# Opening of a fused SSD and MLP kernel: second weight slice in halves between ramps, the long running sum moved forward, one load released a step sooner

## The chip, the core and the metric

The kernel runs on one core of a Trainium2 chip. Its engines are TensorE (PE in the profile; its weight loads have a row of their own, PEld), VectorE (DVE), ScalarE (ACT), GpSimd (POOL) and SyncE (SP), whose queue issues nearly all DMAs here. The metric is the device time of one execution in microseconds; the median of the runs is compared.

## What is computed

First a state-space attention block (4 batches, 8 heads, 768 tokens, head dimension 32, state 16), then an MLP over the 3072 tokens that come out of it (256 wide, 2048 hidden). The core of the reference, cut:

```python
log_a = np.log(np.clip(a, 1e-06, 1.0))
for c in range(nc):                                   # chunks of tokens
    cum = np.cumsum(la, axis=-1)
    L = np.exp(cum[:, :, :, None] - cum[:, :, None, :]) * causal
    M = np.einsum('bhin,bhjn->bhij', Cc, Bc) * L
    y[:, :, sl] = M @ xc + (Cc @ state) * np.exp(cum)[..., None]
    state = np.exp(np.sum(la, -1)) * state + ...      # decayed B^T x of the chunk
x = y.transpose(0, 2, 1, 3).reshape(B * S, H * D)
h = x @ w_in                                          # 3072x256 @ 256x2048
g = h * np.clip(h + 3.0, 0.0, 6.0) / 6.0
out = g @ w_out                                       # 2048x256
```

The two weight matrices arrive as 64-bit floats. [...]

## The kernel before

**Stages.** The tokens are worked on in six chunks of 128 per batch (512 tokens a chunk over the four batches). An opening computes the attention of chunk 0. Then, for each chunk k, comes its MLP, with the attention of the next chunk woven in. The MLP's first half runs over 16 units f of 128 hidden columns. In chunk 0 a unit is `mlp_in` (L711): two matmuls of 128x512 in float32 into one of four PSUM banks (tag `f0` to `f3`, bank f % 4), then a ramp on ACT (`ramp`, L819: relu of h/6 + 1/2 into gT) and the product with h on DVE (`times_ramp`, L824). A bank is free for unit f + 4 when L824 of unit f has read it. `first_out` (L837) multiplies gT with w_out, after the sixteen units.

**Weights.** w_in and w_out come in eight slices of 1 MB, `load_w(0)` to `load_w(7)` (L157), through three buffers named raw; slices 0 to 3 are w_in, and slice i serves the units 4i to 4i + 3. The SP queue issues the loads in order. Load 1 is held back by a memset of one column on DVE (L154): it is called in `multiply` (L642, four products of chunk 0's decays with its scores) behind the second of the four products. Load 2 is held back by a copy of one column on POOL (L156) that reads what load 1 brought.

Decoding a slice, 128x1024 numbers, takes on ACT a copy of the top 16 bits (ws, L246) and two passes that make the exponent out of them (L270, L273), and on DVE the significand in two passes (wm, L249 and L253), two masks (we and ws, L263 and L265), an OR of sign and exponent (L277) and the product that writes the slice (L287). `decode(i)` is a generator of five steps, and `weights(i, n)` advances it by n. Slice 1 is decoded by `decode_halves` (L201): the same passes, with those on the exponent, the OR and the product cut into two halves of 512 columns (L211, L217, L220, L222, L229, L231; the significand L212 and L224 is whole). The first half holds the columns of units 4 and 5, the second those of units 6 and 7.

**The order.** It is written out by hand, and each engine executes its instructions in that order. The main part of the opening ends with `decode_halves(1)`, and so all of slice 1's passes stand ahead of unit 0's ramp on ACT, and ahead of unit 0's L824 on DVE. The 16 units follow:

```python
    for i in range(2, NP + 2):
        for j in range(5):
            weave.setdefault(4 * i - 8 + j, []).append(i)
...
                mlp_in(k, f, lambda: [weights(i, 1) for i in late])
```

so slice 2's copy stands behind unit 0, its masks behind unit 1, and so on to its product in unit 4, ahead of that unit's L824; slices 3, 4 and 5 follow four units apart each.

**The running sum.** `add_up` (L319) is a scan on DVE over the logarithms of a, one row per batch and head. The first 256 columns are summed in the opening. The other 512 are summed behind the 16 units of chunk 0, and what reads them follows: `spread_cum` (L368), `store_rows` (L336, L338), `load_eto` (L358) and `load_decay` (L351) send them through DMA to the later chunks' tiles.

The functions follow as the program had them before, with the line numbers of the profile.

Of the kernel before, what the change touches and what calls it, by code (L numbers as in the profile page):

```python
# [8 lines left out]
FP32 = mybir.dt.float32  # L9
U32 = mybir.dt.uint32  # L10
U16 = mybir.dt.uint16
BF16 = mybir.dt.bfloat16
F32R = mybir.dt.float32r
AF = mybir.ActivationFunctionType
ALU = mybir.AluOpType
# [6 lines left out]
def kernel(  # L22
# [24 lines left out]
    nc = tc.nc  # L47
# [7 lines left out]
    NK = DM // P  # L55
# [78 lines left out]
    NP = 4  # L134
    FP = NF // NP
    w_in = [const.tile([P, NK, FP * P], FP32, name="w_in", tag=f"w{i}") for i in range(NP)]
# [33 lines left out]
    def conceal_in(t, pattern):  # L170
# [16 lines left out]
    bias_hi = const.tile([P, 1], FP32, name="bias_hi")  # L187
    nc.vector.memset(bias_hi, 1151.0 * 2 ** 7)
    bias_lo = const.tile([P, 1], FP32, name="bias_lo")
# [4 lines left out]
        out=head, in_=head, pattern=[[-2 * N, NQ], [-N, 2]], compare_op=ALU.is_ge,  # L194
        fill=0.0, base=0, channel_multiplier=1)
    nc.gpsimd.affine_select(
        out=head, in_=head, pattern=[[2 * N, NQ], [N, 2]], compare_op=ALU.is_ge,
# [3 lines left out]
    def decode_halves(i):  # L201

        n, cut = NK * FP * P, FP * P // 2
        top = raws[i].bitcast(U16).rearrange("p (k f w) -> p k f w", k=NK, w=4)[..., 3]
        lo, hi = (raws[i].rearrange("p (n w) -> p n w", w=2)[:, :, w] for w in range(2))
        s = att.tile([P, n], U16, name="ws").rearrange("p (k f) -> p k f", k=NK)
        e = att.tile([P, n], U16, name="we").rearrange("p (k f) -> p k f", k=NK)
        m = att.tile([P, n], U32, name="wm")
        halves = [slice(h * cut, (h + 1) * cut) for h in range(2)]
        for h in halves:  # L210
            nc.scalar.copy(out=s[:, :, h], in_=top[:, :, h])  # L211
        nc.vector.tensor_scalar(  # L212
            out=m, in0=hi, scalar1=0xFFFFF, scalar2=0x100000,
            op0=ALU.bitwise_and, op1=ALU.bitwise_or)
        for h in halves:
            for t, mask in ((e, 0x7FF0), (s, 0x8000)):
                nc.vector.tensor_scalar(  # L217
                    out=t[:, :, h], in0=s[:, :, h], scalar1=mask, scalar2=None,
                    op0=ALU.bitwise_and)
            nc.scalar.activation(  # L220
                e[:, :, h].bitcast(BF16), e[:, :, h], AF.Relu, bias=bias_hi, scale=-8.0)
            nc.scalar.activation(  # L222
                e[:, :, h], e[:, :, h].bitcast(BF16), AF.Relu, bias=bias_lo, scale=-1.0)
        nc.vector.scalar_tensor_tensor(  # L224
            out=m.bitcast(FP32), in0=lo, scalar=2.0 ** -32, in1=m, op0=ALU.mult, op1=ALU.add)
        load_w(i + NRAW)
        m = m.bitcast(FP32).rearrange("p (k f) -> p k f", k=NK)
        for h in halves:
            nc.vector.tensor_tensor(  # L229
                out=e[:, :, h], in0=e[:, :, h], in1=s[:, :, h], op=ALU.bitwise_or)  # L230
            nc.vector.scalar_tensor_tensor(  # L231
                out=w_in[i][:, :, h], in0=m[:, :, h], scalar=2.0 ** -20,
                in1=e[:, :, h].bitcast(BF16), op0=ALU.mult, op1=ALU.mult)

    def decode(i):

        n = NK * FP * P  # L240
        top = raws[i].bitcast(U16).rearrange("p (n w) -> p n w", w=4)[:, :, 3]
        lo, hi = (raws[i].rearrange("p (n w) -> p n w", w=2)[:, :, w] for w in range(2))
        s = att.tile([P, n], U16, name="ws")
        e = att.tile([P, n], U16, name="we")
        m = att.tile([P, n], U32, name="wm")
        nc.scalar.copy(out=s, in_=top)  # L246

        def significand():
            nc.vector.tensor_scalar(  # L249
                out=m, in0=hi, scalar1=0xFFFFF, scalar2=0x100000,  # L250
                op0=ALU.bitwise_and, op1=ALU.bitwise_or)
            yield
            nc.vector.scalar_tensor_tensor(  # L253
                out=m.bitcast(FP32), in0=lo, scalar=2.0 ** -32, in1=m, op0=ALU.mult,
                op1=ALU.add)
            yield

        parts_m = significand()
        if i == 0:
            next(parts_m)  # L260
            next(parts_m)
        yield
        nc.vector.tensor_scalar(  # L263
            out=e, in0=s, scalar1=0x7FF0, scalar2=None, op0=ALU.bitwise_and)
        nc.vector.tensor_scalar(  # L265
            out=s, in0=s, scalar1=0x8000, scalar2=None, op0=ALU.bitwise_and)
        if i:
            next(parts_m)
        yield
        nc.scalar.activation(e.bitcast(BF16), e, AF.Relu, bias=bias_hi, scale=-8.0)  # L270
        next(parts_m, None)
        yield
        nc.scalar.activation(e, e.bitcast(BF16), AF.Relu, bias=bias_lo, scale=-1.0)  # L273
        if i > 1 and i + NRAW < 2 * NP:
            load_w(i + NRAW)
        yield
        nc.vector.tensor_tensor(out=e, in0=e, in1=s, op=ALU.bitwise_or)  # L277
        if i == 0:
            yield
        m, e = m.bitcast(FP32), e.bitcast(BF16)  # L280
        if i < NP:
            dst = w_in[i]
            m, e = (t.rearrange("p (k f) -> p k f", k=NK) for t in (m, e))
        else:
            dst = w_out[:, (i - NP) * FP:(i - NP + 1) * FP, :]
            m, e = (t.rearrange("p (k f) -> p k f", k=FP) for t in (m, e))
        nc.vector.scalar_tensor_tensor(  # L287
            out=dst, in0=m, scalar=2.0 ** -20, in1=e, op0=ALU.mult, op1=ALU.mult)
# [29 lines left out]
    def add_up(sl):  # L318
        nc.vector.tensor_tensor_scan(  # L319
            out=cum[:, sl], data0=run.rearrange("g c p -> g (c p)")[:, sl], data1=a_sb[:, sl],  # L320
            initial=0.0, op0=ALU.mult, op1=ALU.add)
# [165 lines left out]
    def turn_b(c):  # L487

        t_ps = turn_ps(c, 1)
        transposes(c, 1, t_ps)  # L490
        (nc.scalar.copy if c else nc.vector.tensor_copy)(out=turned(c)[0], in_=t_ps)
# [136 lines left out]
    def multiply(c):  # L628

        if 0 < c < TURN:  # L630
            take(c)
        if c <= TURN:
            mids[c] = mid = att.tile([P, NB, 2 * D], FP32, name="mid", bufs=1)
        if c == 0:
            for t in range(2):
                nc.scalar.activation(
                    mid[:, :, t * D:(t + 1) * D], sps[c][0][:, :, t * D:(t + 1) * D], AF.Copy,
                    scale=parity[:, t:t + 1])
            take(c)
        for q in (2, 0, 1, 3) if c >= TURN else range(NQ):  # L640
            hs = slice(2 * q, 2 * q + 2)
            nc.vector.tensor_tensor(  # L642
                out=Ls[c][:, :, hs], in0=Ls[c][:, :, hs], in1=cbs[c][q], op=ALU.mult)
            if c == 0 and q == 1:
                load_w(1)
            if 0 < c <= TURN and q == 1:
                new_state(mid, sps[c][0], tmps[c])
# [63 lines left out]
    def mlp_in(k, f, between):  # L711
        h = ps.tile([P, TB], FP32, name="h", tag=f"f{f % 4}")
        for j in range(NK):
            n = TB // (1 + (f * NK + j >= NF * NK - 0))
            for t in range(0, TB, n):
                nc.tensor.matmul(  # L716
                    out=h[:, t:t + n], lhsT=w_in[f // FP][:, j, f % FP * P:(f % FP + 1) * P],
                    rhs=yTs[k][:, j].rearrange("p b i -> p (b i)")[:, t:t + n],
                    start=(j == 0 and t == 0), stop=True, skip_group_check=True)
        ramp(k, f, h)  # L720
        between()
        times_ramp(k, f, h)
# [427 lines left out]
    def weights(i, n):  # L1150
        for _ in range(n):
            next(parts[i], None)


    def diff(c, *bs):
        for part in (diff_less, diff_pick):
            for b in bs:
                part(c, b)
# [18 lines left out]
            load_x(0)  # L1177
    first_eto()
    turn_b(0)
    diff(1, 0)  # L1180
    diff(1, 1)
    weights(0, 1)
# [20 lines left out]
    renew(0)  # L1203
    mix(0)
    keep(0)
    decode_halves(1)
    load_bc(1)
    load_x(1)


    weave, t_parts = {}, split_sum()
    for i in range(2, NP + 2):
        for j in range(5):
            weave.setdefault(4 * i - 8 + j, []).append(i)
    weave[NF - 1].append(NP + 2)
    for k in range(NC):
        gTs[k] = ffn.tile([P, NF, TB], FP32, name="gT")
        c, ahead = k + 1, k + 2
        if k == 0:
            for f in range(NF):  # L1220
                late = [i for i in weave.get(f, []) if f == 4 * i - 4]
                mlp_in(k, f, lambda: [weights(i, 1) for i in late])
                for i in weave.get(f, []):
                    if i not in late:
                        weights(i, 1)
                if f in (6, 8):
                    diff_exp(c, f // 2 - 3)
            weights(NP + 1, 1)
            add_up(ends_at[1])
            cum_q = spread_cum()  # L1230
            store_rows()
            load_eto(c)
# [180 lines left out]
```

## Time and profile before

| | us |
|---|---|
| median of 3 runs (lowest, highest) | 338.36 (338.15, 338.55) |
| profiled execution, own time | 337.99 |
| its span, first instruction to last | 336.2 |
| PE busy | 328.2 (98% of the span) |
| DVE busy | 262.7 (78%) |
| ACT busy | 207.8 (62%) |
| POOL busy | 131.3 (39%) |

The profile is of one execution. The granted TensorE clock was 1.00 in it. All times below are microseconds from the start of the span. A row of a timeline has the start, the duration (of the whole group, where it ends in a count), engine, line, operation, output and inputs; in square brackets stands the idle time before it with what ended it. A row of the chain of waits has start, duration, and what the end of the program hung on in that time. Matmuls in float32 leave two records each, so a unit of two matmuls has four.

### The profile page before, as it was taken

Reading aid. Unit: us, or ns where it says so; the run is one execution under the profiler, and the core shown is the slowest. Engines: PE = TensorE matmul, PEld = TensorE weight load, DVE = VectorE, ACT = ScalarE, POOL = GpSimd, SP = SyncE. Lnnn points to the kernel's source line nnn. Section 1 sums busy time; section 2 is a strip of 40 time slices with the busy share of each in tenths; the row PEclk is TensorE's granted clock in tenths of the full one; section 3 lists DMA queues with packets and bytes.
Section 4 is the critical chain, followed back from the end, with each engine's and each line's share of the span. In section 5 each row is a group of like instructions: output and inputs, shape, how many; then the busy total and the mean of one; then the engine's idle time right before and its main releaser. Section 6 shows DMA issues by size and latency. Waiting matters only on the chain.

```text
span 336.2 us, 8336 instructions
## 1 busy us (share of the span) xinstructions
PE 328.2 (98%) x3361; PEld 263.7 (78%) x3361; DVE 262.7 (78%) x419; ACT 207.8 (62%) x450; POOL 131.3 (39%) x126
## 2 busy tenths in 40 slices
PE   6999999999999999999999999999999999999995
PEld 3653358888878888888888888888888888899995
DVE  7787999788699729769949558938678958599973
ACT  3777877658976571677662477643487221677661
POOL 2100000172364799079983078771058750000000
PEclk9999999999999999999999999999999999999999
DMA  6869990492980215239107257100141001110001
GB/s 102 170 220 306 120 338 16 112 136 63 205 108 0 59 26 138 39 59 88 40 2 164 36 79 71 33 4 10 28 72 18 2 4 17 29 20 0 2 0 62
DMA packets 90277, 25.22 MB, mean 75 GB/s; under 512 B 82880, under 2 KB 86624, under 8 KB 89728
## 3 DMA queue, kind: packets, MB, share of 16 engines
q1 hardware_dynamic: 89664, 24.57, 38.4%
q8 instruction: 26, 0.43, 0.6%
q10 hardware_dynamic: 576, 0.13, 0.2%
q14 instruction: 11, 0.09, 0.1%
HBM read 21.33 MB, written 3.29 MB: 73 GB/s over the span
## 4 chain that ended last, share of the span: by engine, by line
PE 81%; DVE 8%; DMA 6%; ACT 2%; issue 1%; SPq 0%; POOL 0%; DVEq 0%; POOLq 0%
PE h L780 29%; PE wc L1028 8%; PE o L837 8%; PE wb L1028 8%; PE wa L1028 7%; PE o_end L992 6%; DMA raw<-in_moe_w_in_dram 5%; PE h L716 4%; PE wb L1036 3%; DVE gT L824 2%; PE y L690 2%; DVE q_part L920 2%; PE y L556 2%; PE cb L587 1%; DVE w_part L752 1%
## 5 line engine op out<-in xcount | busy, mean ns | idle before, releaser
L824 DVE SCALAR_TENSOR_TENSOR gT<-gT,h 128x512 f32<-128x512 f32 x96 | 64.7, 683 | 24.8 <-ACT gT L819 23.3
L819 ACT ACTIVATE gT<-h,half 128x512 f32<-128x512 f32 x96 | 65.0, 685 | 21.5 <-PE h L780 21.4
L800 ACT ACTIVATE h<-h 128x512 f32<-128x512 f32 x66 | 38.2, 585 | 38.0 <-PE h L780 37.7
L780 PE MATMUL h<-y_hi,w_part 128*128 128x512 f32 x160 | 51.6, 407 | 0.5 <-DVE gT L824 0.5
L780 PE MATMUL h<-y_less,w_part 128*128 128x512 f32 x160 | 50.2, 399 | 0.0
L780 PE MATMUL h<-y_lo,w_part 128*128 128x512 f32 x160 | 49.4, 395 | 0.0
L883 POOL TENSOR_TENSOR s<-gT 128x512 f32<-128x512 f32 x16 | 24.9, 1555 | 50.8 <-DVE gT L824 50.8
L780 PEld LDWEIGHTS h<-y_hi,w_part 128*128 128x128 f32 x160 | 29.9, 188 | 7.8 <-DVE gT L824 1.2
L780 PEld LDWEIGHTS h<-y_lo,w_part 128*128 128x128 f32 x160 | 30.0, 188 | 7.3
L780 PEld LDWEIGHTS h<-y_less,w_part 128*128 128x128 f32 x160 | 29.1, 188 | 6.0 <-ACT h L800 0.2
L445 ACT ACTIVATE L<-L,cum_n 128x64 f32<-128x64 f32 x128 | 31.7, 336 | 0.7 <-POOL L L173 0.7
L716 PE MATMUL h<-yT,w_in 128*128 128x512 f32 x64 | 28.8, 600 | 1.2 <-DVE gT L824 1.2
L837 PE MATMUL o<-w_out,gT 128*128 128x256 f32 x128 | 28.8, 381 | 0.0
L837 PEld LDWEIGHTS o<-w_out,gT 128*128 128x128 f32 x128 | 24.1, 190 | 3.8 <-issue 0.5
L716 PEld LDWEIGHTS h<-yT,w_in 128*128 128x128 f32 x64 | 11.6, 189 | 17.6 <-issue 11.5
L883 POOL TENSOR_TENSOR gT<-gT 128x512 f32<-128x512 f32 x16 | 23.9, 1500 | 0.7
L173 POOL TENSOR_SCALAR_AFFINE_SELECT L<-L 64x1024 f32<-64x1024 f32 (+1 forms) x16 | 19.9, 1249 | 7.5 <-DMA L<-cum_d 7.2
L920 DVE TENSOR_TENSOR q_part<-gT,q_part 128x256 fp32r<-128x256 f32 x24 | 21.4, 921 | 0.0
L992 PE MATMUL o_end<-v_pair,g_pair 128*128 128x256 f32 x120 | 21.0, 281 | 0.0
L883 POOL TENSOR_TENSOR s<-s,gT 128x512 f32<-128x512 f32 x16 | 20.5, 1289 | 0.0
L992 PEld LDWEIGHTS o_end<-v_pair,g_pair 128*128 128x128 f32 x120 | 18.8, 189 | 1.2
L456 POOL TENSOR_TENSOR bs<-B,L 128x128 f32<-128x128 f32 x24 | 11.7, 507 | 17.8 <-ACT L L445 12.1
(173 smaller groups left out, 615.7 us busy)
## 6 DMA issues: line engine op xcount, KB each, us to landing
raw<-in_moe_w_in_dram SPq DMA_DIRECT2D x4, 1024.0 KB
raw<-in_moe_w_out_dram SPq DMA_DIRECT2D x4, 1024.0 KB
L<-cum_d SPq DMA_DIRECT2D x8, 512.0 KB
xt<-in_x_dram SPq DMA_DIRECT2D x6, 512.0 KB
out_dram<-back SPq DMA_DIRECT2D x128, 16.0 KB
B<-in_B_dram SPq DMA_DIRECT2D x6, 256.0 KB
eto<-cum_e SPq DMA_DIRECT2D x20, 64.0 KB
pairs<-in_C_dram SPq DMA_DIRECT2D x36, 32.0 KB
```

Of the source, the lines that this page charges most:

```text
L173: nc.gpsimd.affine_select(out=t[rows], in_=t[rows], pattern=pattern, compare_op=ALU.is_ge, fill=-1e5, base=base, channel_multiplier=-1)
L445: nc.scalar.activation(Ls[c][:, b, h], Ls[c][:, b, h], AF.Exp, bias=cum_n[:, c, g:g + 1])
L716: nc.tensor.matmul(out=h[:, t:t + n], lhsT=w_in[f // FP][:, j, f % FP * P:(f % FP + 1) * P], rhs=yTs[k][:, j].rearrange("p b i -> p (b i)" ...
L780: nc.tensor.matmul(out=hs_[k, f], lhsT=w[j][:, f % FP * P:(f % FP + 1) * P], rhs=y[:, j], start=(start and j == 0), stop=True, skip_group_ ...
L800: nc.scalar.activation(h, h, AF.Copy, scale=1.0 / EPS + 1.0)
L819: nc.scalar.activation(gTs[k][:, f], h, AF.Relu, bias=half, scale=1.0 / 6.0)
L824: nc.vector.scalar_tensor_tensor(out=g, in0=g, scalar=1.0, in1=h, op0=ALU.min, op1=ALU.mult)
L837: nc.tensor.matmul(out=o[:, b % 2], lhsT=gTs[0][:, f, b * P:(b + 1) * P], rhs=w_out[:, f], start=(f == 0 and b % 2 == 0), stop=True, skip_ ...
L883: nc.gpsimd.tensor_tensor(out=o, in0=p_, in1=q_, op=op)
L920: nc.vector.tensor_tensor(out=l[:, j], in0=g[:, j], in1=h[:, j].bitcast(FP32), op=ALU.subtract)
L992: nc.tensor.matmul(out=ends_["cross" if n == 2 else "squares"][b], lhsT=g_parts[t][n][:, b * P:(b + 1) * P], rhs=w, start=(t == 0 and b < ...
L1028: nc.tensor.matmul(out=bank[:, slot], lhsT=lhs[:, j], rhs=rhs[:, j], start=(clear and j == 0), stop=True, skip_group_check=True)
```

## The change

Five edits in the same kernel. Names and line numbers are those of before.

1. `load_w(1)`, and with it the memset that releases the second load, is called behind the first of the four products in `multiply`.
2. The scan of the last 512 columns, `add_up(ends_at[1])`, is called in the opening, behind the copy of bT (L491) and ahead of slice 0's decoding, and no longer behind the 16 units.
3. `decode_halves` becomes a generator. Its exponent passes on ACT and its OR and product on DVE are done for the first half, then it pauses; unit 0's ramp and product follow, then the second half's.
4. Slice 2's steps move within the units: the copy (L246) and the first significand pass (L249) to unit 2, between its ramp and its L824; the masks to unit 3; the exponent passes and the second significand pass behind unit 3; OR and product in unit 4 as before.
5. In `decode(2)` the first significand pass stands in the first step, ahead of the masks.

On ACT the order of the pieces concerned was: both halves' exponent passes, ramp 0, copy of slice 2, ramps 1 and 2, exponent pass of slice 2, ramp 3, second pass. It becomes: first half's passes, ramp 0, second half's passes, ramps 1 and 2, copy of slice 2, ramp 3, the two passes of slice 2. On DVE it was: half, half, L824 of units 0 and 1, masks of slice 2, significand, unit 2, significand, unit 3, OR, product, units 4 and 5. It becomes: half, unit 0, half, unit 1, significand, unit 2, masks, unit 3, significand, OR, product, units 4 and 5. PE and POOL keep their order, and the SP queue keeps the order of its DMAs. The new line numbers are 8 to 13 higher: 256, 260, 271, 273, 285, 295 for `decode`, 226, 231, 234, 218, 220 for the halves, 650 for the four products, 827 and 832 for ramp and product of a unit.

```diff
@@ decode_halves
+        def exponents(h):
+            nc.scalar.activation(
+                e[:, :, h].bitcast(BF16), e[:, :, h], AF.Relu, bias=bias_hi, scale=-8.0)
+            nc.scalar.activation(
+                e[:, :, h], e[:, :, h].bitcast(BF16), AF.Relu, bias=bias_lo, scale=-1.0)
+
+        def result(h):
+            nc.vector.tensor_tensor(
+                out=e[:, :, h], in0=e[:, :, h], in1=s[:, :, h], op=ALU.bitwise_or)
+            nc.vector.scalar_tensor_tensor(
+                out=w_in[i][:, :, h], in0=m.bitcast(FP32).rearrange("p (k f) -> p k f", k=NK)[:, :, h],
+                scalar=2.0 ** -20, in1=e[:, :, h].bitcast(BF16), op0=ALU.mult, op1=ALU.mult)
...
         load_w(i + NRAW)
         for h in halves:
+            exponents(h)
+            result(h)
+            yield
@@ decode
         parts_m = significand()
+        if i in (0, 2):
+            next(parts_m)
         if i == 0:
-            next(parts_m)
             next(parts_m)
         yield
...
-        if i:
+        if i not in (0, 2):
             next(parts_m)
@@ multiply
-            if c == 0 and q == 1:
+            if c == 0 and q == 0:
                 load_w(1)
@@ the opening
     turn_b(0)
+    add_up(ends_at[1])
     diff(1, 0)
...
-    decode_halves(1)
+    second = decode_halves(1)
+    next(second)
     load_bc(1)
     load_x(1)
...
-    for i in range(2, NP + 2):
+    for i in range(3, NP + 2):
@@ the 16 units
-                mlp_in(k, f, lambda: [weights(i, 1) for i in late])
+                mlp_in(k, f, lambda: [weights(i, 1) for i in (late or [2] * (f in (2, 3, 4)))])
+                if f == 0:
+                    next(second)
+                if f == 3:
+                    weights(2, 2)
...
             weights(NP + 1, 1)
-            add_up(ends_at[1])
             cum_q = spread_cum()
```

More of the change, by code (lines that the diff above doesn't have):

```diff
@@ L219, in decode_halves @@
                     op0=ALU.bitwise_and)
[L220 to L223, printed above, removed]
         nc.vector.scalar_tensor_tensor(
@@ L226, in decode_halves @@
         load_w(i + NRAW)
-        m = m.bitcast(FP32).rearrange("p (k f) -> p k f", k=NK)
         for h in halves:
[L229 to L233, printed above, removed]
+            exponents(h)
+            result(h)
+            yield
     def decode(i):
```

## Prediction

> **What bounds the kernel now.** I read the page first, then the chain of waits from the opening on, then the timelines of the engines around the place where the chain leaves TensorE.
>
> ```profile
> PE 328.2 (98%) x3361; PEld 263.7 (78%) x3361; DVE 262.7 (78%) x419; ACT 207.8 (62%) x450; POOL 131.3 (39%) x126
> ```
>
> PE is busy for 98% of the span, so time is to be had only where PE stands still or where the opening ahead of its long run gets shorter. The chain (start, duration, what the end hung on) says where:
>
> ```profile
> 15.42 5.21 DMA raw<-in_moe_w_in_dram
> ...
> 20.75 0.65 POOL raw L156
> 21.41 5.25 DMA raw<-in_moe_w_in_dram
> 26.69 1.11 ACT ws L246
> 27.80 0.59 ACT gT L819
> 28.42 0.69 DVE gT L824
> ...
> 33.47 1.23 DVE w_in L287
> 34.70 0.61 DVE gT L824
> 35.35 14.00 PE h L716 x32
> ```
>
> Up to 35.35 the end hangs on loads 1 and 2, on ACT's copy of slice 2 and on DVE; only from 35.35 on it runs on PE. Yet PE had begun its units long before:
>
> ```profile
> 19.31 9.16 PE L716 MATMUL h<-yT,w_in 128*128 128x512 f32 x20
> 29.16 5.71 PE L716 MATMUL h<-yT,w_in 128*128 128x512 f32 x12 [0.69 <-DVE gT L824]
> 20.70 0.19 PEld L716 LDWEIGHTS h<-yT,w_in 128*128 128x128 f32 x1 [0.24 <-issue]
> 24.99 0.19 PEld L716 LDWEIGHTS h<-yT,w_in 128*128 128x128 f32 x1 [0.24 <-issue]
> 26.48 0.30 PEld L716 LDWEIGHTS h<-yT,w_in 128*128 128x128 f32 x2 [0.87 <-DVE gT L824]
> ```
>
> Between the weight loads at 20.70 and 24.99 lie ten matmul records, so one takes 0.429 and a unit of four 1.72. From 19.31 to 35.35 are 16.04 for the 32 records of units 0 to 7, which by that pace take 13.73. **2.31 is lost**, at units 4 (26.48), 5 (29.16) and 8 (35.35), each time waiting for L824, which frees the bank. The cause stands in the chain: at 26.69 ACT begins slice 2's copy, for which it had waited, and ramp 1 stands behind it. Without waits unit 8 begins at 35.35 - 2.31 = 33.04; unit 4 at 26.18, 5 at 27.90, 6 at 29.61, 7 at 31.33, 12 at 39.90, and the output products at 46.8 (estimates). These are the due times below.
>
> **Edits 1 and 2: the second load and the scan.**
>
> ```profile
> 9.70 0.69 DVE L491 COPY bT<-t_ps 128x512 f32<-128x512 f32 x1 [1.14 <-PE t_ps L482]
> 11.42 0.69 DVE L249 TENSOR_SCALAR wm<-raw 128x1024 uint32<-128x1024 uint32 x1 [1.04 <-DMA raw<-in_moe_w_in_dram]
> 14.09 1.89 DVE L642 TENSOR_TENSOR L<-L,cb 128x512 f32<-128x512 f32 x3
> 15.32 0.06 DVE L154 MEMSET raw<- 128x1 uint32 x1
> 17.55 1.23 DVE L287 SCALAR_TENSOR_TENSOR w_in<-wm,we 128x1024 f32<-128x1024 f32 x1
> 55.20 1.21 DVE L319 TENSOR_TENSOR_SCAN rowed<-rowed 32x512 f32<-32x512 f32 x1
> 10.00 0.41 POOL L456 TENSOR_TENSOR bs<-B,L 128x128 f32<-128x128 f32 x1 [0.17 <-ACT L L425]
> ```
>
> DVE ends L491 at 10.39 and then idles 1.04 until load 0 lands. The scan takes 1.21; begun 0.07 before that end, as instructions that don't depend on each other do here (15.32 against 14.09 + two products), it ends at 11.53, and slice 0's L249 begins 0.04 later. That is its whole cost; without the idle time it would be 1.2. The instructions behind it stay that late, and PE's first unit at 19.31 has 0.53 in hand over w_in's first slice (17.55 + 1.23). The memset moves ahead of one product, 0.60: it ends at 14.82, and load 1 goes out 0.56 sooner, at 14.86, on a queue with nothing else before it. It lands at 20.07. POOL's copy follows it by 0.78, load 2 goes out at 20.85 and lands 5.25 later, at **26.10** (before 26.66). Load 3 follows at the same distance as before.
>
> The Trainium skill, "SBUF — State Buffer", section "Who interferes with whom", says that a DVE instruction with two SBUF inputs and a GpSimd instruction that reads SBUF exclude each other for the whole instruction. By that the scan would wait for POOL's L456 until 10.41, 0.09 more than above; the sum below would lose nothing by it, for 0.09 is within the slack of unit 8.
>
> **Edits 3 to 5: halves, ramps, third copy.** What the passes take:
>
> ```profile
> 20.65 0.69 DVE L212 TENSOR_SCALAR wm<-raw 128x1024 uint32<-128x1024 uint32 x1 [0.81 <-DMA raw<-in_moe_w_in_dram]
> 22.47 1.22 DVE L224 SCALAR_TENSOR_TENSOR wm<-raw,wm 128x1024 f32<-128x1024 uint32 x1
> 24.68 0.42 DVE L229 TENSOR_TENSOR we<-we,ws 128x512 uint16<-128x512 uint16 x1
> 25.14 0.69 DVE L231 SCALAR_TENSOR_TENSOR w_in<-wm,we 128x512 f32<-128x512 f32 x1
> 29.02 0.42 DVE L263 TENSOR_SCALAR we<-ws 128x1024 uint16<-128x1024 uint16 x1
> 32.75 0.69 DVE L277 TENSOR_TENSOR we<-we,ws 128x1024 uint16<-128x1024 uint16 x1
> 35.81 0.42 DVE L263 TENSOR_SCALAR we<-ws 128x1024 uint16<-128x1024 uint16 x1
> 20.65 1.25 ACT L211 COPY ws<-raw 128x512 uint16<-128x512 uint16 x2 [0.85 <-DMA raw<-in_moe_w_in_dram]
> 22.55 0.72 ACT L222 ACTIVATE we<-we,bias_lo 128x512 uint16<-128x512 bf16 x1
> 29.48 1.15 ACT L270 ACTIVATE we<-we,bias_hi 128x1024 bf16<-128x1024 uint16 x1 [0.52 <-DVE we L263]
> ```
>
> Instructions that wait for the one ahead begin 0.03 after its end, others up to 0.1 before it. No instruction is added here; all change place. ACT, with load 1 at 20.07: copies 20.09 to 21.34, first half's two passes to 22.71, ramp 0 to 23.29, second half's passes to 24.66, ramps 1 and 2 to 25.80 (PE has units 1 and 2 done by then). Now it waits for load 2 where it used to wait with ramp 1 behind; only ramp 3 is behind it now. Copy 26.13 to 27.24, ramp 3 to 27.81.
>
> DVE: L212 at 20.09, masks, L224 to 23.13; first half's OR and product to 24.19; **unit 0 to 24.80** (due 26.18; its weights at 24.19); second half from 24.70, when ACT has it, to 25.85; **unit 1 to 26.43** (due 27.90). Then slice 2's first significand pass, a new wait for load 2 (26.10, met) with units 2 and 3 queued behind it, to 27.02; **unit 2 to 27.61** (due 29.61); masks 27.51 to 28.40, the copy being there at 27.24; **unit 3 to 28.98** (due 31.33). Significand to 30.10. ACT's two passes run from 27.96 to 30.29, so the OR waits 0.2 and ends at 31.01, the product at 32.27, **unit 4 at 32.85, due 33.04**: slack 0.19, the tightest point. A slice later, DVE does four units and a slice in 6.79 (29.02 to 35.81), PE four units in 6.86. Slice 3 begins at 33.37, unit 8 ends 6.29 later at 39.66 (34.70 + 0.61 - 29.02 = 6.29), due 39.90. w_out's first slice is ready at 40.16 + 5.68 = 45.84, due 46.8.
>
> Every wait goes, by this count, and 2.31 with them. Two due times have only 0.2 in hand, and I take 0.06 off for them. Sum: **2.25**. Were load 2 no sooner, unit 4 would end at 33.2, and the sum would be 2.1: edit 1 alone is worth that little.
>
> The Trainium skill, "DMA: Bandwidth & Descriptors", section "Anatomy of one DMA — SWDGE (gpsimd) path", fits a DMA's time there as 2.0 plus its bytes at 436 GB/s, for 1 MB an estimate of 4.4, against 5.21 and 5.25 in this trace (issued by SP). By that, slice 2 would be there 0.85 sooner and the sum would be 2.31; the measurement decides.
>
> **What follows the units.** The gain stays if the rest still hangs on PE.
>
> ```profile
> 69.20 1.53 POOL L173 TENSOR_SCALAR_AFFINE_SELECT L<-L 64x1024 f32<-64x1024 f32 x1 [0.76 <-DMA L<-cum_d]
> 71.91 3.45 POOL L173 TENSOR_SCALAR_AFFINE_SELECT L<-L 128x1024 f32<-128x1024 f32 x3 [1.19 <-DMA L<-cum_d]
> 69.63 1.64 DVE L752 SCALAR_TENSOR_TENSOR w_part<-w_part,w_in 128x512 fp32r<-128x512 f32 x1
> 72.61 1.29 DVE L642 TENSOR_TENSOR L<-L,cb 128x512 f32<-128x512 f32 x2 [0.62 <-PE cb L587]
> 80.78 1.42 DVE L770 TENSOR_TENSOR y_lo<-yT,y_hi 128x256 fp32r<-128x256 f32 x4
> 83.66 1.28 PE L780 MATMUL h<-y_lo,w_part 128*128 128x512 f32 x4
> 88.68 0.58 ACT L800 ACTIVATE h<-h 128x512 f32<-128x512 f32 x1 [0.22 <-PE h L780]
> ```
>
> It does: at 72.61 DVE waits for PE, at 88.68 ACT does, where the chain leaves PE next. The output products need DVE's slices of w_out, and DVE comes as much sooner as PE, then 1.21 more by the scan that is gone. What reads the scan goes out on SP right behind the last load, and no longer waits for the scan's end at 56.41; POOL's passes L173, which waited for its DMA, come sooner too. I cost this part at nothing; it is covered by DVE's 0.62, and what it costs if the cover is gone is the second rival. So the profiled execution of 337.99 would come to 335.74; the median of the runs lies 0.37 above that execution, 338.36, and I forecast **336.1** on it.
>
> **The rivals.** (1) *Slice 2 still comes last.* The passes from load 2's landing to unit 4's L824 add up to 6.5 with nothing between, so a landing later than 26.5, or DVE held for more than 0.2 on the way, shifts unit 8 one for one. For it: two slacks of 0.2 out of a count with some thirty instructions. Against it: the same instructions have kept their durations over all slices. With 1.2 lost, the gain is 1.1: **337.3**.
>
> (2) *DVE is held behind the units.* POOL's four passes (4.98) may now run beside DVE's split of w_in. One such meeting stands in the trace: L752 at 69.63 takes 1.64 and not 0.69, while POOL runs from 69.20. DVE would have 0.62 + 1.21 = 1.8 in hand at L642; if all 4.98 stood in its way and not only the 0.95 of now, it would be 2.2 late, of which y_lo's slack (83.66 - 82.20 = 1.46) takes up most: 0.8 lost, **336.9**. To give back the whole gain it would take more than POOL's passes hold. The same section of the Trainium skill as above gives this rule, the lock for the whole instruction; the row at 69.63 agrees.
>
> (3) *Slower: the loads share the rate.* Loads 2 and 3 go out one right behind the other, now as before. If they were served side by side, load 2 would land up to 5.2 later, which is what a load takes by itself. Unit 2's and 3's L824 now stand behind slice 2's pass on DVE, so units 6 and 7 would wait with unit 8. The change is slower from a landing after 26.5 + 2.3 = 28.8; with the whole 5.2, at 31.3, PE loses 4.8 where it lost 2.3: **340.9**. Against it: load 2 took 5.25 with load 3 behind it, load 1 took 5.21 with none.
>
> (4) *More comes.* With DVE freer by 1.21 and the decays sooner, a wait behind the units may shrink too, say by 0.5: **335.6**.
>
> **How the numbers follow.** Chances: forecast 0.62, rival (1) 0.18, (2) 0.11, (3) 0.04, (4) 0.05. The range goes from 335.5, with (4) in it, to 337.3; outside are the worse part of (1) and (2), 0.12, (3), and a little beyond (4), together under 0.2. A change of 0.2%, 0.7 us, is about what a measurement of this kernel can tell from none. Faster by more: 0.62 + 0.05 and most of (1) and (2), 0.15 + 0.07, is 0.89. Within it: the rest of those two, 0.07. Slower: 0.04.
>
> **What would show it.** In the changed kernel's profile load 1 should go out at about 14.9 and load 2 at 20.9; no idle time <-DVE gT should stand ahead of L716's records; the sixteen units should run from 19.3 to about 46.8; unit 4's L824 should end near 32.9; DVE should do the scan between 10.3 and 11.6. The later waits should keep their names and lie 2.2 to 2.3 sooner: L642 near 70.3, L800 near 86.4. I am wrong if load 2 doesn't land near 26.1, if DVE's pieces between 20 and 33 take longer in their new order, or if the units gain and the span doesn't.

## The result: 2.5 to 3.7 us less, more than forecast

The median of the changed kernel is 335.20 us (334.93 to 335.46, 4 runs) against 338.27 (338.15 to 338.55, 4 runs) of the kernel before beside it. The ratio is 0.9908, 95% interval [0.9891, 0.9925]: 2.5 to 3.7 us faster. Two more comparisons, on other runs, gave 0.9914 [0.9899, 0.9929] and 0.9916 [0.9901, 0.9931]. Forecast were 336.1 and the range 335.5 to 337.3; the time lies 0.3 below the range. The profiled execution took 335.13, its span 333.4 (before 337.99 and 336.2).

From the page of the changed kernel, the busy times and the chain by engine:

```profile
PE 327.6 (98%) x3361; PEld 264.6 (79%) x3361; DVE 262.1 (79%) x419; ACT 208.0 (62%) x450; POOL 131.8 (40%) x126
...
PE 98%; POOL 0%; ACT 0%; issue 0%; DVE 0%; POOLq 0%
```

The busy times are those of before within 1 us. What changed is the chain: in this execution it runs on PE for 98% of the span, from the opening to the end (in two more of the same kernel for 86% and 92%, with the same stages, so the share alone says little). So the question is which waits of PE have gone. PE's timeline after, at the borders of the stages:

```profile
19.44 27.82 PE L724 MATMUL h<-yT,w_in 128*128 128x512 f32 x64
...
81.65 1.28 PE L788 MATMUL h<-y_lo,w_part 128*128 128x512 f32 x4
...
96.69 0.63 PE L788 MATMUL h<-y_hi,w_part 128*128 128x512 f32 x2
...
102.72 1.89 PE L1036 MATMUL wa<-gT,w_out 128*128 128x256 f32 x8
```

The sixteen units are one group of 64 records with no wait that the profile names; before, they were three groups with waits for L824 between them. The other rows belong to the second stage that changed. From chunk 1 on, a unit multiplies parts of the tokens (y_hi, y_lo, y_less) with parts of w_in (w_part); DVE and ACT make the parts of w_in slice by slice, which is called the split below. The stage runs from chunk 1's first products with y_lo to its first products `wa` with w_out. Of before, these rows of PE's timeline weren't shown yet:

```profile
49.19 13.98 PE L837 MATMUL o<-w_out,gT 128*128 128x256 f32 x64
...
99.43 0.73 PE L780 MATMUL h<-y_hi,w_part 128*128 128x512 f32 x2 [0.48 <-DVE gT L824]
...
105.56 1.89 PE L1028 MATMUL wa<-gT,w_out 128*128 128x256 f32 x8
```

A fourth wait for L824 stands at 99.43. The same record comes after at 96.69, without a wait. It stands 15.77 behind the first y_lo group before (83.66, in the prediction) and 15.04 after: by there, 0.73 of the loss has fallen, of which the profile names 0.48 as a wait. The stages, cut at PE's marks in the profiled executions (first unit; first output product, at 47.10 after; first y_lo group; first wa):

| us | before | after | difference |
|---|---|---|---|
| opening, to the first unit | 19.31 | 19.44 | +0.13 |
| sixteen units of chunk 0 | 29.88 | 27.66 | -2.22 |
| output products, attention of chunk 1 | 34.47 | 34.55 | +0.08 |
| **chunk 1, y_lo to wa** | 21.90 | 21.07 | **-0.83** |
| all the rest | 230.64 | 230.68 | +0.04 |

The units gave 2.22, forecast 2.25. The 0.83 lies in a stage that begins more than 60 us after the units do, and that the prediction costed at nothing.

What happened there shows on DVE and POOL. DVE before, while it splits the last slice of w_in into parts (L752 and L755, two inputs each) between the units' L824:

```profile
92.62 1.08 DVE L752 SCALAR_TENSOR_TENSOR w_part<-w_part,w_in 128x512 fp32r<-128x512 f32 x1
93.73 1.51 DVE L755 TENSOR_TENSOR w_part<-w_part 128x512 fp32r<-128x512 f32 x1
95.17 1.27 DVE L824 SCALAR_TENSOR_TENSOR gT<-gT,h 128x512 f32<-128x512 f32 x2
96.36 1.69 DVE L752 SCALAR_TENSOR_TENSOR w_part<-w_part,w_in 128x512 fp32r<-128x512 f32 x1
98.09 0.69 DVE L755 TENSOR_TENSOR w_part<-w_part 128x512 fp32r<-128x512 f32 x1
```

DVE after, the same instructions:

```profile
90.62 0.68 DVE L760 SCALAR_TENSOR_TENSOR w_part<-w_part,w_in 128x512 fp32r<-128x512 f32 x1
91.34 1.67 DVE L763 TENSOR_TENSOR w_part<-w_part 128x512 fp32r<-128x512 f32 x1
92.93 1.27 DVE L832 SCALAR_TENSOR_TENSOR gT<-gT,h 128x512 f32<-128x512 f32 x2
94.13 0.68 DVE L760 SCALAR_TENSOR_TENSOR w_part<-w_part,w_in 128x512 fp32r<-128x512 f32 x1
94.84 0.69 DVE L763 TENSOR_TENSOR w_part<-w_part 128x512 fp32r<-128x512 f32 x1
```

Three of the four passes were long before, one is after. POOL before at that time:

```profile
89.66 1.14 POOL L173 TENSOR_SCALAR_AFFINE_SELECT L<-L 64x1024 f32<-64x1024 f32 x1 [2.79 <-DMA L<-cum_d]
92.02 4.23 POOL L173 TENSOR_SCALAR_AFFINE_SELECT L<-L 128x1024 f32<-128x1024 f32 x3 [1.21 <-DMA L<-cum_d]
96.22 1.28 POOL L883 TENSOR_TENSOR s<-gT 128x512 f32<-128x512 f32 x1
```

and POOL after:

```profile
84.84 5.13 POOL L173 TENSOR_SCALAR_AFFINE_SELECT L<-L 64x1024 f32<-64x1024 f32 x4
90.79 1.67 POOL L891 TENSOR_TENSOR s<-gT 128x512 f32<-128x512 f32 x1 [0.83 <-DVE gT L832]
```

These are the passes that take chunk 3's upper triangle out (`conceal_in`); L883 is an addition over gT. Before, they waited twice for a DMA with the running sums (`L<-cum_d`), and so three of the four ran from 92.02 to 96.25, beside DVE's split. After, they are done at 89.97, before the split begins at 90.62; only L891 meets it. The lengths fit one rule: a DVE pass that meets a POOL instruction ends 0.55 after that instruction does (before, L752 at 98.05 and L883 at 97.50; after, L763 at 93.01 and L891 at 92.46), as if it ran only then. The two long passes ahead of them before end 0.53 after POOL's first and second L173 of the three (93.17 and 94.71).

Why the sums came sooner is on SP's queue. Before:

```profile
56.44 2.73 SPq L368 DMA_DIRECT2D cum_q<-rowed  x4
...
68.90 9.28 SPq L110 DMA_DIRECT2D pairs<-in_C_dram  x8
...
83.51 2.09 SPq L351 DMA_DIRECT2D L<-cum_d  x2
```

and after:

```profile
44.45 2.78 SPq L376 DMA_DIRECT2D cum_q<-rowed  x4
...
65.98 6.24 SPq L110 DMA_DIRECT2D pairs<-in_C_dram  x8
...
77.54 1.78 SPq L359 DMA_DIRECT2D L<-cum_d  x2
```

With the scan in the opening, the DMAs of the sums go out 11.99 sooner. The loads of chunk 2's decays go out at 55.39 and no longer at 63.98, just ahead of `pairs`; those eight DMAs are issued in 6.24 instead of 9.28, and the load for chunk 3 goes out 5.97 sooner, where PE is only 2.0 sooner by then.

### The profile page after: what moved, and what is told of

Same layout as the page of the kernel before. It is cut to its first block, busy times and chain, and to the rows that moved or that the text cites. A ratio compares the mean times of both kernels' runs of the same rounds, so it can differ in the third digit from the quotient of the medians.

```text
span 333.4 us, 8336 instructions
## 1 busy us (share of the span) xinstructions
PE 327.6 (98%) x3361; PEld 264.6 (79%) x3361; DVE 262.1 (79%) x419; ACT 208.0 (62%) x450; POOL 131.8 (40%) x126
## 4 chain that ended last, share of the span: by engine, by line
PE 98%; POOL 0%; ACT 0%; issue 0%; DVE 0%; POOLq 0%
PE h L788 33%; PE wb L1036 9%; PE wc L1036 8%; PE o L845 8%; PE h L724 8%; PE wa L1036 8%; PE o_end L1000 6%; PE wb L1044 3%; PE y L698 2%; PE y L564 2%; PE cb L595 2%; PE d L403 1%; PE d L425 1%; PE y L618 1%; PE sp L618 1%; PE d L416 1%
## 5 line engine op out<-in xcount | busy, mean ns | idle before, releaser
L891 POOL TENSOR_TENSOR s<-gT 128x512 f32<-128x512 f32 x16 | 25.3, 1581 | 54.1 <-DVE gT L832 54.1
L724 PE MATMUL h<-yT,w_in 128*128 128x512 f32 x64 | 27.8, 595 | 0.0
L891 POOL TENSOR_TENSOR gT<-gT 128x512 f32<-128x512 f32 x16 | 23.9, 1501 | 0.7
L724 PEld LDWEIGHTS h<-yT,w_in 128*128 128x128 f32 x64 | 12.0, 190 | 15.1 <-issue 13.2
L173 POOL TENSOR_SCALAR_AFFINE_SELECT L<-L 64x1024 f32<-64x1024 f32 (+1 forms) x16 | 20.1, 1264 | 1.7 <-DMA L<-cum_d 1.2
L891 POOL TENSOR_TENSOR s<-s,gT 128x512 f32<-128x512 f32 x16 | 20.6, 1298 | 0.0
L464 POOL TENSOR_TENSOR bs<-B,L 128x128 f32<-128x128 f32 x24 | 11.6, 502 | 20.7 <-ACT L L453 14.7
```

The lines of the kernel that those rows point to most:

```text
L173: nc.gpsimd.affine_select(out=t[rows], in_=t[rows], pattern=pattern, compare_op=ALU.is_ge, fill=-1e5, base=base, channel_multiplier=-1)
L724: nc.tensor.matmul(out=h[:, t:t + n], lhsT=w_in[f // FP][:, j, f % FP * P:(f % FP + 1) * P], rhs=yTs[k][:, j].rearrange("p b i -> p (b i)" ...
L891: nc.gpsimd.tensor_tensor(out=o, in0=p_, in1=q_, op=op)
```

## The experiments

**Theory.** The units gain what was counted. The extra 0.83 comes from the scan, and not from DVE's freed 1.21 but from the DMAs behind it: POOL's passes for chunk 3 no longer stand beside DVE's split. **Rival A:** the scan helps because DVE is freer by 1.21 behind the units; the DMAs don't matter. **Rival B:** the extra comes with the reordered decoding or the load, not with the scan.

The table has all profiles, cut at the same marks, and the gain in time as the ratio gives it, in us of 338, with its interval. Between executions the opening alone varies from 19.09 to 19.81, in kernels with the early scan as in those without; the stages are therefore the sharper measure.

| kernel | opening | units | to y_lo | y_lo to wa | gain (95%) |
|---|---|---|---|---|---|
| before | 19.31 | 29.88 | 34.47 | 21.90 | |
| after | 19.44 | 27.66 | 34.55 | 21.07 | 3.1 (2.5, 3.7) |
| after, second | 19.42 | 27.74 | 34.36 | 21.07 | 2.9 (2.4, 3.4) |
| after, third | 19.25 | 27.57 | 34.63 | 21.07 | 2.8 (2.4, 3.3) |
| e1 scan only | 19.81 | 30.00 | 34.44 | 21.07 | 0.5 (0.2, 0.8) |
| e2 no scan | 19.72 | 28.10 | 34.40 | 21.85 | 1.8 (1.3, 2.3) |
| e3 halves only | 19.31 | 28.46 | 34.52 | 21.80 | 1.5 (0.9, 2.0) |
| e4 DMAs held | 19.41 | 27.58 | 34.33 | 21.73 | 2.2 (1.7, 2.7) |
| e5 load only | 19.19 | 29.72 | 34.44 | 22.17 | 0.4 (0.0, 0.8) |
| e6 without load | 19.09 | 28.35 | 34.44 | 21.07 | 2.2 (1.7, 2.7) |
| e7 passes called later | 19.54 | 30.10 | 34.51 | 21.43 | -0.2 (-0.5, 0.2) |
| e8 passes left out | 19.14 | 30.21 | 34.33 | 21.07 | 0.9 (0.6, 1.2) |
| e9 load first | 19.67 | 27.57 | 34.48 | 21.11 | 2.9 (2.5, 3.4) |

**e1: before, with the scan alone moved.**

```diff
     turn_b(0)
+    add_up(ends_at[1])
     diff(1, 0)
...
-            add_up(ends_at[1])
             cum_q = spread_cum()
```

> The kernel before with the long scan moved into the opening and nothing else. Theory (DMA): the scan's results go out some ten us sooner, GpSimd's concealment passes for chunk 3 (L173) are done before VectorE splits w_in's last slice, these splits take 0.69 each and not up to 1.7, and TensorE's wait in chunk 1's units (0.48 idle, 0.8 in all) goes: 0.8 us faster than before, with the first sixteen units still losing 2.3. Rival A (VectorE freed of 1.21 us is what counts): also 0.8 faster, so this run does not part A from the theory. Rival B (the 0.8 came with the units' own gain, by another phase): no change, within 0.2.

Measured 337.63 against 338.01, ratio 0.9986 [0.9977, 0.9995]. The second stage is 21.07: the 0.83 are there with the scan alone, and rival B falls. The time gained less, 0.5; in the profiled execution the opening was 0.5 longer than that of before. 0.8 is at the interval's end.

**e2: the changed kernel with the scan put back** (the same lines the other way).

> The changed kernel with the long scan back behind the sixteen units. Theory (DMA) and rival A: the units keep their gain of 2.2, the 0.8 in chunk 1's units is gone again: 2.2 to 2.3 faster than before, and the wait for VectorE of about 0.5 stands in chunk 1's units as it did. Rival B: 3.0 faster, as the whole change.

Measured 336.25, ratio 0.9947 [0.9932, 0.9961]. The second stage is 21.85, and PE waits there again for DVE:

```profile
97.94 0.73 PE L788 MATMUL h<-y_hi,w_part 128*128 128x512 f32 x2 [0.48 <-DVE gT L832]
```

So among the five edits the scan is needed for this gain, and enough for it. The gain of 1.8 (1.3 to 2.3) lies under the 2.2 to 2.3 expected, which its interval only just reaches: the units took 28.10 here, 0.26 of it a wait at unit 8, since load 2 was there only at 27.36.

**e3: before, with the three edits of the decoding alone** (no early scan, `load_w(1)` behind the second product).

> The kernel before with the halves, the ramps and the third copy in their new order; scan and second load as before. Load 2 lands near 26.7; unit 8 starts at about 33.4 to 33.5 and the units gain 2.0 to 2.2. Theory (DMA) and rival A: 2.0 to 2.2 faster than before. Rival B: 2.8 to 3.0 faster.

Measured 336.82, ratio 0.9957 [0.9942, 0.9972]: 1.5, under the 2.0 to 2.2 expected. ACT's copy of slice 2 (L253 in the changed kernel, L246 before), and behind it the row of PE:

```profile
27.31 1.16 ACT L253 COPY ws<-raw 128x1024 uint16<-128x1024 uint16 x1 [0.92 <-DMA raw<-in_moe_w_in_dram]
```

```profile
33.94 14.00 PE L724 MATMUL h<-yT,w_in 128*128 128x512 f32 x32 [0.63 <-DVE gT L832]
```

In the chain of waits of this kernel, load 2 stands with a longer time than the 5.25 of before, and at the same start:

```profile
21.43 5.86 DMA raw<-in_moe_w_in_dram
```

So the new order has no reserve against a late load, which is what rival (1) of the prediction said. The late load isn't all of it: this kernel lacks edit 1, and what that alone costs is under e6.

**e4: the changed kernel, with the DMAs of the sums held to their old place.** A copy of one column of `cum` onto itself on DVE is all that is added; what reads `cum` waits for it.

```diff
             weights(NP + 1, 1)
+            nc.vector.tensor_copy(cum[:, 2 * P:2 * P + 1], cum[:, 2 * P:2 * P + 1])
             cum_q = spread_cum()
```

> The changed kernel, but a one-column copy of the running sum onto itself on VectorE at the old place of the scan, so that VectorE is free of the scan's 1.21 us there but the DMAs that read the sum cannot go out before (about 53). Theory (DMA): GpSimd's passes for chunk 3 fall beside the splits again, 0.5 of idle time comes back in chunk 1's units: 2.2 to 2.4 faster than before. Rival A (VectorE freed): 3.0 faster, as the whole change.

Measured 335.94, ratio 0.9935 [0.9920, 0.9950]. The units took 27.58, as in the changed kernel, but the second stage is 21.73. DVE is as free as in the changed kernel, the sums are as early, and only the DMAs are late: rival A falls. POOL, DVE and PE of this kernel:

```profile
89.12 3.79 POOL L173 TENSOR_SCALAR_AFFINE_SELECT L<-L 128x1024 f32<-128x1024 f32 x3 [1.70 <-DMA L<-cum_d]
```

```profile
90.29 1.62 DVE L760 SCALAR_TENSOR_TENSOR w_part<-w_part,w_in 128x512 fp32r<-128x512 f32 x1
91.94 1.51 DVE L763 TENSOR_TENSOR w_part<-w_part 128x512 fp32r<-128x512 f32 x1
```

```profile
94.10 0.73 PE L788 MATMUL h<-y_hi,w_part 128*128 128x512 f32 x2 [0.36 <-DVE gT L832]
```

**e7: before, with the calls of chunk 3's passes moved from units 3 and 7 to units 10 and 13**, to take them away from the split.

```diff
-            if f in ((3, 7)) and ahead < NC:
-                conceal(ahead, int(f == 7))
+            if f in ((10, 13) if k == 1 else (3, 7)) and ahead < NC:
+                conceal(ahead, int(f == (13 if k == 1 else 7)))
```

> Before with one thing changed: POOL's passes L173 for chunk 3 are called in units 10 and 13 of chunk 1, not 3 and 7, so that they are not beside DVE's split of w_in's last slice. My theory (they hold DVE's L752 and L755, and with them the y_lo that PE waits for): both lines take 0.69 each there, the stall of 0.48 on PE is gone, the stage takes 21.1 and the kernel is 0.8 faster, with everything of the change left out. Rival (the late decays themselves, by another way than DVE's split): 21.9 as before, no change, or slower by up to 1 because chunk 3's decays come later still.

Measured 337.95, ratio 1.0005 [0.9995, 1.0015]: no change. But it didn't do what it was meant to. POOL has nothing else to do there and goes by the DMA, not by the place in the program:

```profile
89.31 1.14 POOL L173 TENSOR_SCALAR_AFFINE_SELECT L<-L 64x1024 f32<-64x1024 f32 x1 [1.94 <-DMA L<-cum_d]
91.66 3.79 POOL L173 TENSOR_SCALAR_AFFINE_SELECT L<-L 128x1024 f32<-128x1024 f32 x3 [1.21 <-DMA L<-cum_d]
95.42 1.71 POOL L883 TENSOR_TENSOR s<-gT 128x512 f32<-128x512 f32 x1
```

POOL was 0.8 earlier than before when it came to L883, and DVE's third pass met nothing any more; that stage took 21.43, between the two. POOL, SP and PE ran their instructions in the same order as before, so for this stage it is one more execution of the kernel before, and it decides nothing about the cause. What it shows is the scatter: with the DMAs late the stage took 21.43 to 22.17 in six profiles, with them early 21.07 to 21.11 in six. The 0.83 is the difference of one pair of executions; the means, 21.81 and 21.08, lie 0.74 apart.

**e8: before, with these four passes left out.**

```diff
-            if f in ((3, 7)) and ahead < NC:
+            if f in ((3, 7)) and ahead < NC and k > 1:
```

> Before with POOL's four passes L173 for chunk 3 left out (the part of the scores above the diagonal is then not taken out in that chunk); nothing else, and the decays stay as late as they were. Theory (POOL's passes beside DVE's split of w_in's last slice hold it up, and that is what the early scan removes): L752 and L755 at 92 to 98 take 0.69 each, but for one beside POOL's L883; PE's 0.48 <-DVE gT is gone; the stage takes 21.1 instead of 21.9 and the kernel is 0.8 faster (0.6 to 1.0), 2.3 less than the change gives. Rival (the late decays cost by another way, say through ACT's exponentials or the DMAs): the stage stays at 21.9, 0 to 0.1 faster.

Measured 336.99 against 337.77, ratio 0.9974 [0.9964, 0.9983]: 0.8 by the medians. DVE:

```profile
92.65 0.68 DVE L752 SCALAR_TENSOR_TENSOR w_part<-w_part,w_in 128x512 fp32r<-128x512 f32 x1
93.37 1.67 DVE L755 TENSOR_TENSOR w_part<-w_part 128x512 fp32r<-128x512 f32 x1
...
96.16 0.68 DVE L752 SCALAR_TENSOR_TENSOR w_part<-w_part,w_in 128x512 fp32r<-128x512 f32 x1
96.87 0.69 DVE L755 TENSOR_TENSOR w_part<-w_part 128x512 fp32r<-128x512 f32 x1
```

The sums are as late as before, every edit of the change is missing, and with POOL's passes alone gone the stage takes 21.07, to the hundredth that of the changed kernel. The one long pass stands beside L883, as after. The part of the scores above the diagonal stays in for that chunk, so this kernel is for the time alone.

**e5: before, with the second load's release alone moved.**

```diff
-            if c == 0 and q == 1:
+            if c == 0 and q == 0:
                 load_w(1)
```

> Before with the second load's release alone moved. The chain of before hangs on that load from 15.42 to 35.35. My theory: load 2 lands at about 26.1 and not 26.66, the chain behind it is as it was, the units take 29.3 and not 29.9, and the kernel is 0.5 faster; the second stage stays at 21.9. Rival: the load's time in flight grows when it goes out sooner (beside the last work of the opening), or DVE's halves set the chain: nothing, 0.

Measured 337.52 against 337.71, ratio 0.9988 [0.9976, 1.0001]: from nothing to 0.8. The load went out 0.56 sooner but was under way for 5.47 instead of 5.21, by the chain of waits of this kernel,

```profile
14.86 5.47 DMA raw<-in_moe_w_in_dram
```

so slice 2 came 0.28 sooner (ACT's copy at 26.41 and not 26.69), and the units took 29.72. The expected 0.5 was too much; the direction can't be told from none.

**e6: the changed kernel with the second load behind the second product.**

> The changed kernel with the second load released behind the second product again. By the sum on record unit 4's product then ends 0.15 behind its due time, and it is 0.15 slower than the changed kernel, about 2.9 faster than before. Rival, after the run without scan and load: load 2 stays under way for longer (landing at 27.3) and unit 8 waits 0.6, so it is 0.6 slower than the changed kernel, about 2.5 faster than before. The second stage keeps its 21.1 in both.

Measured 335.52, beside 334.96 of the changed kernel on the same chip: 0.56 slower. The rival's size, and yet not its reason. Load 2 was not late here (ACT's copy began at 26.77 and DVE's first pass on it at 26.98, without a wait). DVE's timeline shows what is last, its run over slice 1:

```profile
20.72 0.69 DVE L226 TENSOR_SCALAR wm<-raw 128x1024 uint32<-128x1024 uint32 x1 [0.91 <-DMA raw<-in_moe_w_in_dram]
...
26.98 0.69 DVE L256 TENSOR_SCALAR wm<-raw 128x1024 uint32<-128x1024 uint32 x1
...
31.00 0.69 DVE L285 TENSOR_TENSOR we<-we,ws 128x1024 uint16<-128x1024 uint16 x1 [0.20 <-ACT we L281]
...
32.87 1.28 DVE L832 SCALAR_TENSOR_TENSOR gT<-gT,h 128x512 f32<-128x512 f32 x2
```

From load 1's landing to unit 4's product (32.87 + 0.68 = 33.55) DVE has one short wait; that is 12.83, and 12.82 in the changed kernel (20.39 to 33.21). Unit 8 therefore comes as much later as **load 1** does. Counted from PE's first unit, DVE begins on load 1 after 1.63 here and after 1.00 in the second execution of the changed kernel; the units took 0.61 longer here than there. PE's unit 8:

```profile
33.60 14.00 PE L724 MATMUL h<-yT,w_in 128*128 128x512 f32 x32 [0.51 <-DVE gT L832]
```

**e9: the changed kernel with that load ahead of the first product**, to see whether more is to be had there; beside it the changed kernel a third time.

```diff
+        if c == 0:
+            load_w(1)
         for q in (2, 0, 1, 3) if c >= TURN else range(NQ):
...
-            if c == 0 and q == 0:
-                load_w(1)
```

> The changed kernel with the second load released ahead of the first product, one product sooner still. Theory (with the changed order load 2 is the tight point only by a few tenths): load 2 goes out 0.3 to 0.6 sooner, unit 8 waits no more (0.2 in one profile of the changed kernel), and it is 0 to 0.3 faster than the changed kernel. Rival (load 2 still bounds units 8 and on): 0.5 faster. If the memset, or the load beside the rest of the opening's traffic, gets in the way: slower by up to 0.3.

> The changed kernel beside the next two on one chip: 2.5 to 3.4 faster than before, units in 27.6 to 27.9, the stage behind chunk 1's y_lo in 21.1.

Measured 334.86 and 334.92, the same. Slice 2's copy began at 25.75 and waited for nothing, and the units took 27.57 in both: 64 records at the 0.429 of the prediction need 27.5, so hardly anything is left, and the load no longer bounds. The second run of the changed kernel stood beside e5 to e7:

> The changed kernel once more, beside the next three on the same chip. As the first time: 2.5 to 3.7 faster than before; units in 27.6 to 27.9, the stage behind chunk 1's y_lo in 21.1. If the 0.83 of the second stage were chance, it would be 21.9 there.

It took 334.96, with 27.74 and 21.07 in the two stages.

## Why the prediction was wrong, and where it was right

**The loss in the units: right.** 2.25 forecast, 2.22 measured; all three waits are gone, and no new one is named in their place.

**The path to it: later by 0.2 to 0.4 throughout.** Load 1 went out at 15.1, not 14.9, and slice 2's copy began at 26.50, not 26.13; unit 4's product ended at 33.21, not 32.85. The opening itself was later in that execution (bT's copy at 10.02, not 9.70), and the scan and slice 0's first pass behind it. PE's first unit came 0.13 later too, which was luck, and the slack of 0.19 took up most of the rest: by the table's best units, 27.57, about 0.09 was lost, where 0.06 had been taken off.

**The scan: its price right, its cover gone.** It was to stand in DVE's idle time until load 0 lands. In this execution the load was there at 11.18, while the scan held DVE until 11.83, and slice 0's first pass began at 11.76. The memset that releases load 1 begins 3.26 to 3.30 behind that pass in all five profiles that release load 1 as the change does, so load 1 went out 0.58 later than its load 0 would have allowed, and 0.25 later than forecast; the slack above took most of that up. The opening lost nothing that shows, because it hung on PE: the openings with early scan go down to 19.09, those without to 19.14. POOL's L464 was still running when the scan began (until 10.75), and the scan took 1.20, as long as before: the 0.09 that the prediction names beside its sum doesn't show.

**"Edit 1 alone is worth that little" (0.15): wrong.** It is worth 0.56 (e6). The sum looked only at load 2 and its 6.5 to unit 4's product. DVE's run over slice 1 begins at load 1 and takes 12.8 to the same point, and it is the longer path as soon as load 2 is on time: by the prediction's own numbers 20.65 + 12.76 = 33.41, or 0.37 late and not 0.16. In e6's profile it is 0.73 late: the product ended 0.14 later than that, and PE's first unit came 0.22 sooner. The total didn't suffer, since the edit was in.

**"I cost this part at nothing": the step that failed.** The prediction said that the rest hangs on PE and named L800 at 88.68 as the place "where the chain leaves PE next". It took that row for a wait of 0.22 that would only come sooner. It didn't read on to see when the chain comes back to PE. The chain of waits of before has, behind that row,

```profile
92.70 1.01 DVE w_part L752
...
93.73 1.51 DVE w_part L755
...
96.44 1.63 DVE w_part L752
...
99.43 6.29 PE h L780 x26
```

For almost 11 us, from 88.68 to 99.43, the end hung on ACT and DVE, with DVE's long passes in the middle and PE's lost time at the end. The term put at nothing measured 0.83 in this pair of profiles (0.74 by the means under e7): by the medians the gain is 3.07 where 2.25 was forecast. The other 0.09 by which the forecast of 336.1 missed is the kernel before, at 338.27 beside the change and not at 338.36. A wait that a DMA sets (POOL's 2.79 and 1.21 for `L<-cum_d`) goes when the DMA goes sooner, and the prediction had itself said that these passes would come sooner. But it looked only for where they would arrive (its rival (2), beside the split ahead of L642) and not for what they would leave behind. Both happened. At 65.98 and 67.65 two of DVE's passes now take 1.63 and 1.52 beside POOL's L173, and DVE still waits 1.39 for PE before L650, at 70.56: rival (2) cost nothing. At 92 the same meeting was undone, and gave 0.83.

Rival (4), "a wait behind the units may shrink too", had the direction, with 0.5 instead of 0.83, no place, and a chance of 0.05. The decays that come sooner were the reason (e1, e4, and e8 for how they act); DVE's freed 1.21, which it named beside them, was not (e4).

The Trainium skill, "SBUF — State Buffer", section "Who interferes with whom", says that a DVE instruction with two SBUF inputs contends with a GpSimd instruction that reads SBUF for a port pair that is an exclusive lock. It says that the first to issue holds the pair for its whole instruction, though of DVE's two-port modes. The traces agree with both for these passes: ends 0.53 to 0.55 apart, and 0.69 again when the other is taken away (e8). The rule stood in the prediction, in rival (2), for another pair of rows.

**Not settled:** why SP issues the eight `pairs` in 6.24 after and 9.28 before. In e4, where the loads for chunk 2 again go out shortly before, it is 9.05; over all profiles it is 5.99 to 6.51 with these loads early and 8.52 to 9.58 with them late. That they hold the queue fits, but nothing tried it alone. Open too is load 2 in e2 and e3, the two kernels with the new order and the late scan: from the end of POOL's copy that releases it to ACT's copy of slice 2 it took 6.08 and 5.91, and 5.17 to 5.45 in the ten other profiles where ACT waits for it. That can be chance, or the kernel.

## What to carry to other kernels

Follow the chain of waits from the edit to the end of the span, and at each place where it leaves the bounding engine read on to where it returns: what lies between is time that an edit far upstream can free. If an edit moves a DMA sooner, look at what its readers do beside other work now, and not only at what they will meet in their new place. And where two engines share a path, a pass of two or three times its usual length in one profile is a price that can be read off directly.

## What the runs showed of the hardware

**A copy of one column that takes 0.64 or 0.19.** POOL's copy that releases load 2 begins 0.1 after DVE's first pass over slice 1 and ends as that pass does. In the changed kernel:

```profile
20.48 0.64 POOL L156 COPY raw<-raw 128x1 uint32<-128x1 uint32 x1 [9.74 <-DMA raw<-in_moe_w_in_dram]
```

and in e9, where DVE was still busy with an earlier instruction when load 1 landed:

```profile
20.01 0.19 POOL L156 COPY raw<-raw 128x1 uint32<-128x1 uint32 x1 [9.04 <-DMA raw<-in_moe_w_in_dram]
```

All other profiles have 0.64. So most of the 0.78 that the prediction allowed from load 1's landing to load 2's release fits waiting for DVE; nothing else was tried on it.

**A load's time under way.** 1 MB took 5.21 and 5.25 in the profile of before, 5.47 (e5, load 1), 5.86 (e3, load 2) and 6.03 (e2, load 2) in others, with the same loads behind it. A slack of 0.2 behind such a load isn't one to rely on.
